# Layer 1's second product by 2x2 blocks in seven products, and attention by pairs of tiles

## The chip, the cores and the metric

The kernel runs on one core of a Trainium2 chip. Its time is the device time of one execution in microseconds: 808.15, the median of three runs (807.37 to 808.33). The engines are called as the profile calls them: PE (matrix products), PEld (its weight loads), DVE and ACT (elementwise work), POOL, and SP, which here issues all DMAs. TensorE's granted clock is at its upper level (2.4 GHz) in all but the very ends of the span.

## The reference

Attention within chunks of 64 tokens, and then two feed-forward layers on 2304 tokens:

```
scores = q k^T / 8  in chunks of 64;  attn = softmax(scores);  x = attn v   # 4 x 8 heads x 576 x 64 -> 2304 x 512
h = x @ w_in;   r = max(h, 0);   g = s*(r*r) + b;   y = g @ w_out           # layer 1: 512 -> 2048 -> 512
h = y @ w2_in;  g = max(h, 0) + log1p(exp(-|h|));   out = g @ w2_out        # layer 2, softplus
```

All is float32. The weights arrive as 64-bit words and are taken apart on the chip (`convert`: load, shift and mask on DVE, a linear step on ACT, three more on DVE).

## The kernel before

Precision. A float32 operand is split into a high part (rounded, ACT, line 584) and a low part (the rest, DVE, line 593). A product is three matmuls: high x high, high x low, low x high, each 128 x 128 by 384 columns.

Tiles. A tile is 128 tokens, a unit (u) two tiles, a group (j) three units, so a matmul's 384 columns are one group's half. `N` is 384.

First product of a layer (`quad`, PE at line 1000): by 2x2 blocks in seven products (Strassen's way with shared sums). For a pair of feature blocks `i` (8 of them) and a group `j` (3) a quad makes seven products of six matmuls; copies between PSUM banks on ACT (`seed`, 1022) and subtractions on DVE (571) stand between them. The four results pass relu or softplus (`hidden`, 1032) into places `go` in SBUF, from where they are stored.

Second product of layer 1 (`block`, PE at 1179): plain, six blocks of 16 features x 4 outputs x 3 matmuls. The features are loaded back (`hid`), squared on ACT (1148), scaled by s and shifted by b on ACT or DVE (436, 438), split, and multiplied. Second product of layer 2 (`second_by_blocks`, PE at 1335): seven products; for these a quad of layer 2 makes four sums of its results, stores seven blocks (`summed`), and `weights2` makes sums of the weights on POOL and stores them too (`forms2`).

Attention (`attention(t)`, one tile at a time): scores on PE (815, 64 columns of q against two heads' keys, where the keys of the other half are zeros), maximum on DVE, exp on ACT, in the first six tiles head by head with the sum beside it, division on POOL (899), transposes (915) and products with the values (934) on PE, and then the forms of a unit for the seven products.

Order. Nothing is scheduled by hand: `Work` takes every operation with a due time (`key`, corrected by the numbers of `TUNE`) and a cost, and writes one fixed order for each engine. Each engine then runs its list in order and waits on semaphores. Where the planner sees a gap of PE at the start, `warmed` puts in matmuls on zeros (line 1502).

Of the kernel before, what the change touches and what calls it, by code (L numbers as in the profile page):

```python
# [18 lines left out]
P = 128  # L19
# [18 lines left out]
ENDING = [(NF - 2, 0), (NF - 2, 1), (NF - 2, 2), (NF - 1, 2), (NF - 1, 0), (NF - 1, 1)]  # L38
ENDING_BY_GROUPS = [(c, j) for j in (2, 0, 1) for c in (NF - 2, NF - 1)]
BLOCKS = [4, 5, 0, 1, 2, 3]  # L40

EARLY = 6
# [10 lines left out]
B_AT = {1: 0, 2: 1, 3: 2, 5: 3, 6: 4, 7: 5, 4: 6}  # L53
# [19 lines left out]
AT_W2 = 0  # L73
AT_GH = 5 * XS
NGH = 4
AT_GL = AT_X2
NGL = 3
AT_Y = AT_GL + NGL * 4 * N

AT_V = AT_Y  # L80
NV = 12


TUNE = {
# [56 lines left out]
class Work:  # L141
# [11 lines left out]
    BYTES = 300e3  # L153
# [11 lines left out]
    def add(self, engines, key, emit, deps=(), uses=(), size=0, after=()):  # L165

        kind, self.nth = f"{self.part}.{self.nth}", self.nth + 1  # L170
        key += TUNE.get(self.turn, 0.0) + TUNE.get(kind, 0.0)
# [12 lines left out]

    def order(self, places):
# [14 lines left out]
        def earliest(op, e):  # L200
# [5 lines left out]
            for u in op.takes:  # L206
                t = max(t, min(free[u.kind].values(), default=float("inf")))
# [86 lines left out]
def block_attention_two_layers(  # L294
# [39 lines left out]
    if tc:  # L334
# [3 lines left out]
        operands = const.tile([P, AT_X2 + AT_WF - AT_W1], F32R, name="operands")  # L338
        shared = []
# [6 lines left out]
        nought = const.tile([P, P], F32R, name="nought")  # L346
        s_sb = const.tile([P, 1], F32, name="s_sb")
        b_sb = const.tile([P, 1], F32, name="b_sb")
        small = [
            [const.tile([P, H, 2], F32, name=f"{x}{i}") for x in ("mx", "sm")]  # L350
            for i in range(4)
        ]
        hid = [
            [dram.tile([P, NM, N], F32, name=f"hid{ph}_{x}") for x in range(2 * NG)]
            for ph in range(1)
        ]
        spill = [dram.tile([P, NM, DM], F32, name=f"spill{ph}") for ph in range(1)]
        summed = {
            (n, j): dram.tile([P, NF, N], F32, name=f"summed{n}_{j}")
# [3 lines left out]
        forms2 = dram.tile([P, 7, NF, 256], F32, name="forms2")  # L363

    def mem(a, n, v=None):

        if a < AT_X2:
            return operands[:, a : a + n].bitcast(F32)
        if a >= AT_WF:
            return plain[:, a - AT_WF : a - AT_WF + n]  # L370
        if a >= AT_W1:
            a -= AT_W1 - AT_X2
            return operands[:, a : a + n].bitcast(F32)
        while len(shared) <= v:
            kind = F32R if len(shared) % 2 else F32
# [1196 lines left out]
```

## Time and profile before

| | |
|---|---|
| median of three runs | 808.15 us |
| the profiled execution | 807.7 us |
| its span | 805.9 us |
| PE busy | 797.4 us, 5191 matmul records |
| DVE, ACT, POOL busy | 637.8, 510.1, 140.6 us |
| DMA | 180.28 MB, mean 224 GB/s |

PE's first attention matmul starts at 7.48 us, the first of a quad at 49.83, layer 1's second product at 249.92, layer 2's first matmul after it at 450.43, and the last matmul at some 801.6. Times of a row are the start and the length of an instruction or of a run of like ones; the next one can start before the last has ended, so a rate is read from starts. In rows of attention a matmul of the program shows as two records (float32 without the split).

### The profile page before, as it was taken

What the parts mean: (1) busy time and instruction counts of PE and PEld (TensorE: products, weight loads), DVE (VectorE), ACT (ScalarE), POOL (GpSimd) and SP (SyncE); (2) the same over time, 40 slices, a digit from 0 to 9 for tenths busy, and PEclk for the clock granted to TensorE, in tenths of its full rate; (3) what the DMA queues carried; (4) which work ended last, traced back from release to release, by engine and by line L of the source; (5) the groups of instructions that cost most, each with busy time, mean ns of one, the idle gap of its engine ahead of it and who ended that gap; (6) DMA issues with size and microseconds to landing.
All of it is one profiled execution on the core that took longest, in us unless ns stands there. A gap on an engine that the chain in (4) does not pass through costs nothing.

```text
span 805.9 us, 14677 instructions
## 1 busy us (share of the span) xinstructions
PE 797.4 (99%) x5191; PEld 780.1 (97%) x5191; DVE 637.8 (79%) x1166; ACT 510.1 (63%) x1085; POOL 140.6 (17%) x162
## 2 busy tenths in 40 slices
PE   8999999999999999999999999999999999999998
PEld 6788999999999999999999999999999999999997
DVE  5999898988868978889946786898865777778864
ACT  5756866666658777776676764655555566555553
POOL 3444411111110112222212320213100000000000
PEclk9999999999999999999999999999999999999999
DMA  8865367878769666777540056766778997678851
GB/s 256 248 179 160 138 210 261 278 245 274 246 227 383 235 202 194 253 222 252 166 136 29 30 191 212 260 227 225 256 261 286 345 347 241 233 236 289 282 176 60
DMA packets 80634, 180.28 MB, mean 224 GB/s; under 512 B 9008, under 2 KB 53040, under 8 KB 79664
## 3 DMA queue, kind: packets, MB, share of 16 engines
q1 hardware_dynamic: 80560, 179.34, 66.9%
q8 instruction: 41, 0.67, 0.4%
q14 instruction: 33, 0.27, 0.1%
HBM read 111.15 MB, written 68.16 MB: 222 GB/s over the span
## 4 chain that ended last, share of the span: by engine, by line
PE 95%; DVE 3%; ACT 1%; issue 0%; POOL 0%; ACTq 0%; POOLq 0%; DVEq 0%
PE at L1000 20%; PE S L1000 13%; PE at L1179 9%; PE S L1179 9%; PE A L1000 9%; PE S L1335 8%; PE at L1335 8%; PE A L1179 6%; PE A L1335 5%; PE S L1502 2%; PE at L934 2%; PE at L815 1%; PE at L915 1%; DVE operands L593 1%; ACT last L839 0%
## 5 line engine op out<-in xcount | busy, mean ns | idle before, releaser
L571 POOL TENSOR_TENSOR mem<-mem 128x256 f32<-128x256 f32 x120 | 104.8, 883 | 377.6 <-DVE mem L551 279.9
L593 DVE TENSOR_TENSOR operands<-mem,operands 128x384 fp32r<-128x384 f32 (+4 forms) x186 | 126.3, 695 | 38.4 <-ACT operands L584 36.8
L593 DVE TENSOR_TENSOR operands<-last,operands 128x384 fp32r<-128x384 f32 (+2 forms) x184 | 111.2, 625 | 46.7 <-ACT operands L584 39.7
L584 ACT CAST operands<-mem 128x384 fp32r<-128x384 f32 (+4 forms) x186 | 111.7, 621 | 55.6 <-PE at L1335 36.0
L584 ACT CAST operands<-last 128x384 fp32r<-128x384 f32 (+2 forms) x184 | 93.5, 528 | 57.8 <-PE S L1179 23.1
L1000 PE MATMUL at<-operands 128*128 128x384 f32 x624 | 120.1, 336 | 0.4 <-ACT S L1022 0.4
L1000 PEld LDWEIGHTS at<-operands 128*128 128x128 f32 x624 | 109.4, 188 | 0.8 <-ACT S L1022 0.7
L1335 PE MATMUL at<-operands 128*128 128x384 f32 x384 | 87.2, 334 | 0.0
L1335 PE MATMUL S<-operands 128*128 128x384 f32 x384 | 87.2, 334 | 0.0
L1179 PE MATMUL at<-operands 128*128 128x384 f32 x432 | 84.5, 335 | 0.9 <-ACT operands L584 0.8
L1000 PE MATMUL S<-operands 128*128 128x384 f32 x420 | 83.6, 336 | 0.0
L1179 PE MATMUL S<-operands 128*128 128x384 f32 x432 | 83.1, 334 | 0.0
L1179 PEld LDWEIGHTS at<-operands 128*128 128x128 f32 x432 | 75.5, 188 | 1.9 <-ACT operands L584 1.1
L1032 ACT ACTIVATE mem<-S 128x384 f32<-128x384 f32 x104 | 51.0, 492 | 38.8 <-PE S L1000 29.3
L1179 PEld LDWEIGHTS S<-operands 128*128 128x128 f32 x432 | 75.6, 188 | 0.0
L1000 PEld LDWEIGHTS S<-operands 128*128 128x128 f32 x420 | 73.6, 188 | 0.3 <-issue 0.2
L571 DVE TENSOR_TENSOR mem<-mem 128x384 f32<-128x384 f32 (+1 forms) x108 | 61.0, 573 | 14.3 <-ACT mem L1032 10.8
L1335 PEld LDWEIGHTS S<-operands 128*128 128x128 f32 x384 | 68.4, 188 | 0.0
L1335 PEld LDWEIGHTS at<-operands 128*128 128x128 f32 x384 | 68.4, 188 | 0.0
L1000 PE MATMUL at<-last,operands 128*128 128x384 f32 x336 | 65.7, 335 | 0.0
L1000 PE MATMUL A<-operands 128*128 128x384 f32 x300 | 60.2, 339 | 0.4 <-DVE A L571 0.4
L1000 PEld LDWEIGHTS at<-last,operands 128*128 128x128 f32 x336 | 58.8, 188 | 0.0
(80 smaller groups left out, 1226.1 us busy)
## 6 DMA issues: line engine op xcount, KB each, us to landing
mem<-in_w_dram SPq DMA_DIRECT2D x64, 512.0 KB, 4.6
summed<-mem SPq DMA_DIRECT2D x168, 192.0 KB, 2.5
mem<-summed SPq DMA_DIRECT2D x30, 768.0 KB, 5.5
hid<-mem SPq DMA_DIRECT2D x96, 192.0 KB, 3.0
last<-hid SPq DMA_DIRECT2D x24, 768.0 KB, 5.0
last<-summed SPq DMA_DIRECT2D x12, 768.0 KB, 5.2
mem<-forms SPq DMA_DIRECT2D x7, 1024.0 KB, 6.6
last<-in_q_dram SPq DMA_DIRECT2D x18, 256.0 KB, 4.7
```

The costliest lines, as they stand in the source:

```text
L571: lambda e: on(e).tensor_tensor(out=out(), in0=x(), in1=y(), op=op or ALU.subtract),
L584: lambda e: nc.scalar.copy(out=hi().bitcast(F32R), in_=x()),
L593: lambda e: nc.vector.tensor_tensor(out=lo().bitcast(F32R), in0=x(), in1=hi(), op=ALU.subtract),
L815: nc.tensor.matmul(out_[c * D : (c + 1) * D, pr], of("q")[:, pr * P + c * D : pr * P + (c + 1) * D], kb[:, :, pr, c, :], start=True, stop= ...
L915: nc.tensor.transpose(at(pt)[:, c], of("e")[:, c], ident)
L934: nc.tensor.matmul(at(px)[y, x], of("v")[y, x], of("aT")[y, x], start=True, stop=True)
L1000: nc.tensor.matmul(acc(dst)().rearrange("p (u c) -> p u c", u=GROUP), l[a], r[c], start=start and kk == 0 and x == 0, stop=kk == 1 and x == 2,
L1032: lambda e: nc.scalar.activation(out=at(go), in_=acc(place)(), func=AF.Softplus if ph else AF.Relu),
L1179: nc.tensor.matmul(at(accs[d])[:, :N], l[a], r[c], start=m == 0 and z == 0, stop=m == NM - 1 and z == 2,)
L1335: nc.tensor.matmul(at(accs[d])[:, :N], l[a], r[c], start=i == 0 and y == 0, stop=i == NF - 1 and y == 2,)
L1502: nc.tensor.matmul(x, nought, nought.unsqueeze(1).to_broadcast([P, KK, P]), start=True, stop=True)
```

## The change

Layer 1's second product uses `second_by_blocks` too, with seven products. `quad` makes squares (ACT) of its four results in layer 1 and then the four sums, on POOL for the first two feature blocks and on DVE for the rest; all seven blocks are stored. s is applied where results leave PSUM. b times the sum of the weights' columns is made by two columns of ones beside the first product's right operand (`more`), and added by ACT (`biased`). The weights' forms of layer 1 are made and stored as those of layer 2 are, the sums now on DVE. In the new quads the third and fourth sum are written over a feature, once that feature's store is through. `block`, `hid` and `spill` go away.

Attention runs by units: two tiles together, scores as 64 x 64 products in two PSUM banks, the first half of the heads of every unit with exp head by head. The low parts of six units' sums, 1024 wide, are made on POOL. In part of the weight conversions (`SIGNED`) ACT carries the sign through two steps, and DVE has one step less. Places in SBUF, `TUNE` and the lookahead are new, so every engine's order changes.

```diff
-ENDING = [(NF - 2, 0), (NF - 2, 1), (NF - 2, 2), (NF - 1, 2), (NF - 1, 0), (NF - 1, 1)]
...
-BLOCKS = [4, 5, 0, 1, 2, 3]
-
-EARLY = 6
+ENDING = [(c, j) for j in (2, 0, 1) for c in (NF - 2, NF - 1)]
+
+EARLY = [(u, 0) for u in range(9)]
+BY_PE = []
+LOW_BY_PE = []
+LOW_BY_POOL = range(6)
+SIGNED = [(0, 0), (0, 1), (1, 1)]
...
+SUMS_BY = ["POOL"] * 2 + ["DVE"] * 6
...
-    "attention 1": 3.5, "attention 14": 87, "attention 15": 11, "attention 16": -14, "attention 3": 6,
...
+    "attention 0": -425.5, "attention 0/0": -645, "attention 0/16": 5, "attention 1": -590.5,
...
-    BYTES = 300e3
+    BYTES = 330e3
...
+            if not ph:
+                o = add(
+                    {"ACT": act(N)},
+                    key + 0.1,
+                    lambda e: nc.scalar.activation(out=at(go), in_=at(go), func=AF.Square),
+                    [o],
+                    [go],
+                )
+            return go, o
...
+        t1 = Place(kinds[4])
+        t2, t4 = b11[0], b21[0]
+        e = "DVE" if ph else SUMS_BY[i]
...
+        o1 = sub(key, of(t1), of(b12), of(b11), N, [b12[1], b11[1]], [b12[0], b11[0], t1], e=e)
+        o3 = sub(key, of(b12), of(b22), of(b12), N, [o1, b22[1]], [b12[0], b22[0]], e=e)
+        o2 = sub(
+            key, of(t2), of(b12), of(b11), N, [o3, st1], [b12[0], b11[0], t2], ALU.add, e=e
+        )
+        o4 = sub(
+            key, of(t4), of(b21), of(t2), N, [o2, st2], [b21[0], t2, t4], e=e
+        )
...
+            def scores(e, t=t, primed=primed):
...
+                for pr in range(NP):
+                    for c in range(2):
+                        x = pr * P + c * D
+                        z = t * 256 + (pr % 2 * 2 + pr // 2) * D
+                        for hp in range(2):
+                            y = slice(hp * D, (hp + 1) * D)
+                            nc.tensor.matmul(
+                                at(scores_in[hp])[c * D : (c + 1) * D, z : z + D],
+                                of("q", t)[y, x : x + D],
+                                of("k", t)[y, x : x + D],
...
-                    r = [mem(*hi).bitcast(F32R), mem(*lo).bitcast(F32R)]
+                    r = [mem(hi[0], N + more, version).bitcast(F32R), mem(*lo, version).bitcast(F32R)]
...
+                                nc.vector.scalar_tensor_tensor(
+                                    out=a, in0=ps(), scalar=s_sb[:, 0:1], in1=b, op0=ALU.mult, op1=ALU.add
+                                )
...
-    for z, x in enumerate(BLOCKS):
-        block(0, x // 2, x % 2, end + z * dt, z == 0)
+    late = second_by_blocks(0, end)
```

The orders below are rows of one engine's list: line, operation, out<-in, width, and how many alike.

PE at the start. Before: scores at line 815, transposes 915, values 934, zeros 1502.

```order
L1502 MATMUL S_69<-nought 128x512 x3
L815 MATMUL at_72<-last_121 64x128 x8
L1502 MATMUL S_69<-nought 128x512 x8
L915 MATMUL at_70<-ident,last_121 128x128 x4
L1502 MATMUL S_69<-nought 128x512 x4
L815 MATMUL at_71<-last_121 64x128 x8
L934 MATMUL at_70<-last_121 64x64 x16
```

Now, at the first unit's transposes: scores at line 847, transposes 978, zeros 1566.

```order
L847 MATMUL at_72<-region_0_150 64x64
L847 MATMUL at_71<-region_0_150 64x64
L1566 MATMUL S_69<-nought 128x512 x4
L978 MATMUL at_70<-ident,region_0_143 128x128 x4
L1566 MATMUL S_69<-nought 128x512 x3
L978 MATMUL at_71<-ident,region_0_143 128x128 x4
L1566 MATMUL S_69<-nought 128x512 x6
```

A unit's two banks are transposed one after the other with zeros between. In all, zeros stand 74 times before and 113 times now, 71 and 110 of them ahead of the first matmul of a quad. Ahead of that matmul stand 11 tiles' scores, 9 tiles' transposes and values before, and five units (10 tiles) of each now.

DVE in layer 1's second product. Before: scale and shift (438), splits of features (593), conversions (479 to 551).

```order
L438 TENSOR_SCALAR last_2621<-last_2621,s_sb,b_sb 128x384
L593 TENSOR_TENSOR operands<-last_2621,operands 128x384 x2
L551 SCALAR_TENSOR_TENSOR mem<-mem 128x512
L479 TENSOR_SCALAR mem<-mem 128x512
L509 TENSOR_SCALAR mem<-mem 128x512
L537 SCALAR_TENSOR_TENSOR mem<-mem 128x512
L523 SCALAR_TENSOR_TENSOR mem<-mem 128x512
L593 TENSOR_TENSOR operands<-last_2621,operands 128x384 x2
```

Now: splits of weights and features (625), additions out of PSUM with s (1446), conversions (483 to 583).

```order
L625 TENSOR_TENSOR operands<-region_2_3305,operands 128x3x256
L625 TENSOR_TENSOR region_2_2993<-region_2_3305,region_2_2993 128x384 x4
L1446 SCALAR_TENSOR_TENSOR mem<-S_68,s_sb,mem 128x384
L625 TENSOR_TENSOR region_2_2993<-region_2_3305,region_2_2993 128x384
L1446 SCALAR_TENSOR_TENSOR mem<-at_70,s_sb,mem 128x384
L625 TENSOR_TENSOR region_2_2993<-region_2_3004,region_2_2993 128x384
L499 TENSOR_SCALAR mem<-mem 128x512
```

Additions and weights' splits have come between the features' splits. From the first take out of PSUM (1426) to the last addition (1446) there are 331 DVE instructions: 206 of width 384, 78 of 512 (26 of them TENSOR_SCALAR), 38 of 256, 7 of 768, 2 of 1024.

DVE late in layer 1's first product, with the semaphores that each row waits for (DMAHW is a DMA queue's). Before:

```order
L551 SCALAR_TENSOR_TENSOR mem<-mem 128x512 [waits DVE_49]
L571 TENSOR_TENSOR mem<-at_71,mem 128x384 [waits PE_49]
L479 TENSOR_SCALAR mem<-mem 128x512 [waits DMAHW1_49,DVE_49]
L509 TENSOR_SCALAR mem<-mem 128x512
```

Now: a quad's sums (603, 384 wide), weights' sums (603, 256 wide) and a conversion (583).

```order
L603 TENSOR_TENSOR mem<-mem 128x384 [waits DMAHW3_49,Activation_49]
L583 SCALAR_TENSOR_TENSOR mem<-mem 128x512 [waits DVE_49,Activation_49]
L603 TENSOR_TENSOR mem<-mem 128x384 [waits DVE_49]
L603 TENSOR_TENSOR mem<-mem 128x256 [waits DMAHW5_49]
L603 TENSOR_TENSOR mem<-mem 128x384 [waits DMAHW4_49,DVE_49]
L603 TENSOR_TENSOR mem<-mem 128x256
L603 TENSOR_TENSOR mem<-mem 128x384 [waits DMAHW7_49,DVE_49]
```

Sums of features stand where there were none, and each quad has some that wait for a DMA. By engine, the instructions of one execution go from 1168 to 1320 on DVE, 1039 to 1171 on ACT, 167 to 151 on POOL, 549 to 634 on SP.

## Rows read from the trace of the kernel before

**Rows 1.** The page: busy time by engine, and the chain that ended last.

```profile
PE 797.4 (99%) x5191; PEld 780.1 (97%) x5191; DVE 637.8 (79%) x1166; ACT 510.1 (63%) x1085; POOL 140.6 (17%) x162
...
PE 95%; DVE 3%; ACT 1%; issue 0%; POOL 0%; ACTq 0%; POOLq 0%; DVEq 0%
```

**Rows 2.** Busy by stretch, lines 1179, 1335: stretch, PE, PEld, clock, DMA share, GB/s.

```profile
249.00:451.00 202.00, 200.50 (x1152) 199.57 (x1152) 1.00 0.59 193
...
624.00:806.00 182.00, 175.21 (x1008) 174.76 (x1008) 1.00 0.72 246
```

**Rows 3.** Timeline of PE at the start: start us, length us, instructions.

```profile
30.95 1.89 PE L1502 MATMUL S<-nought 128*128 128x512 f32 x7
...
33.16 0.71 PE L1502 MATMUL S<-nought 128*128 128x512 f32 x2
33.81 1.09 PE L815 MATMUL at<-last 128*64 128x128 f32 x16
34.83 1.15 PE L934 MATMUL at<-last 64*64 64x64 f32 x32
35.91 0.49 PE L1502 MATMUL S<-nought 128*128 128x512 f32 x1
...
49.83 1.31 PE L1000 MATMUL A<-operands 128*128 128x384 f32 x6
```

**Rows 4.** Busy by stretch, line 1502 (matmuls on zeros), columns as Rows 2.

```profile
0.00:60.00 60.00, 22.16 (x74) 13.53 (x74) 1.00 0.80 228
```

**Rows 5.** Timeline of PE: the longest waits after the start, and the last matmuls.

```profile
249.92 0.44 PE L1179 MATMUL at<-operands 128*128 128x384 f32 x1 [0.78 <-ACT operands L584]
...
460.38 1.32 PE L1000 MATMUL at<-operands 128*128 128x384 f32 x6 [0.42 <-ACT S L1022]
...
463.10 1.33 PE L1000 MATMUL A<-operands 128*128 128x384 f32 x6 [0.36 <-DVE A L571]
...
801.28 0.69 PE L1335 MATMUL at<-operands 128*128 128x384 f32 x3
```

**Rows 6.** Timelines of DVE near 702 us and of ACT near 258 us.

```profile
700.62 0.56 DVE L593 TENSOR_TENSOR operands<-mem,operands 128x384 fp32r<-128x384 f32 x1 [0.48 <-ACT operands L584]
701.66 0.56 DVE L593 TENSOR_TENSOR operands<-mem,operands 128x384 fp32r<-128x384 f32 x1 [0.48 <-ACT operands L584]
702.14 0.55 DVE L571 TENSOR_TENSOR last<-S,last 128x384 f32<-128x384 f32 x1
702.61 0.55 DVE L571 TENSOR_TENSOR last<-at,last 128x384 f32<-128x384 f32 x1
...
257.93 0.52 ACT L584 CAST operands<-last 128x384 fp32r<-128x384 f32 x1
258.35 0.52 ACT L1148 ACTIVATE last<-last 128x384 f32<-128x384 f32 x1
```

**Rows 7.** Groups by line and shape: count, busy us, mean ns, idle before.

```profile
L593 DVE TENSOR_TENSOR operands<-last,operands 128x384 fp32r<-128x384 f32 x144 | 84.1, 601 | 35.7 <-ACT operands L584 34.7
...
L537 DVE SCALAR_TENSOR_TENSOR mem<-mem 128x512 uint32<-128x512 uint32 x64 | 45.6, 712 | 1.4 <-ACT mem L496 1.4
```

**Rows 8.** Busy by stretch: PE, PEld, DVE, ACT, POOL, clock, DMA share, GB/s.

```profile
100.00:150.00 50.00, 50.00 (x290) 49.99 (x289) 45.79 (x79) 31.91 (x63) 10.27 (x12) 1.00 0.72 237
...
250.00:300.00 50.00, 49.85 (x286) 49.59 (x287) 45.43 (x84) 41.05 (x86) 7.25 (x8) 1.00 0.72 252
```

**Rows 9.** Line 571 by engine: shortest, median, longest ns; first and last start us.

```profile
L571 POOL TENSOR_TENSOR mem<-mem x120: 725/908/1529, 11.8 to 584.4; 128x256 f32<-128x256 f32 x120
L571 DVE TENSOR_TENSOR mem<-mem x108: 409/555/1089, 74.7 to 633.0; 128x384 f32<-128x384 f32 x96, 128x256 f32<-128x256 f32 x12
```

**Rows 10.** DMA: page's 40 slices; 100 to 250 us (columns as Rows 2); landing of `hid`.

```profile
GB/s 256 248 179 160 138 210 261 278 245 274 246 227 383 235 202 194 253 222 252 166 136 29 30 191 212 260 227 225 256 261 286 345 347 241 233 236 289 282 176 60
...
100.00:250.00 150.00, 149.15 (x859) 148.81 (x857) 1.00 0.76 255
...
DMA to landing us min/median/max: 1.8/3.1/8.9
```

More of the change, by code (lines that the diff above doesn't have):

```diff
@@ L205, in earliest @@
                 t = max(t, d.start)
-            for u in op.takes:
-                t = max(t, min(free[u.kind].values(), default=float("inf")))
+            for x, u in enumerate(op.takes):
+                spots = sorted(free[u.kind].values())
+                nth = sum(o.kind == u.kind for o in op.takes[:x])
+                t = max(t, spots[nth] if nth < len(spots) else float("inf"))
             for u in op.gives:
@@ L456, in block_attention_two_layers, with convert @@
     turn = {}
-    def convert(ph, c, part, key, dst, uses=(), w=(), gone=()):
+    w2_gone = []
+    subtracted = []
+    w1_given = {}
+    def convert(ph, c, part, key, dst, uses=(), w=(), gone=(), ahead=False):
         chain = "f", part
@@ L473, in convert @@
         words = lambda: at(f).bitcast(U32).rearrange("p (a b) -> p a b", b=2)
-        a = lambda: at(am)[:, :DM].bitcast(U32)
-        m = lambda: at(am)[:, DM:].bitcast(U32)
+        a = lambda: at(am).bitcast(U32)
+        m = lambda: dst().bitcast(U32)
+        signed = (ph, part) in SIGNED and not (ph and c >= 2 * LATE)
         o1 = add(
@@ L568, in sub @@
         return add(
-            {e: pool(n) if e == "POOL" else dve(n, port=port)},
+            {z: pool(n) if z == "POOL" else dve(n, port=port) for z in e.split()},
             key,
@@ L577, in sub, with split @@
         )
-    def split(key, hi, lo, x, n, deps, uses=(), psum=False, r=(), wh=(), wl=()):
+    def split(key, hi, lo, x, n, deps, uses=(), psum=False, r=(), wh=(), wl=(), low="DVE"):
         o1 = add(
@@ L590, in split @@
         o2 = add(
-            {"DVE": dve(n, port=not psum)},
+            {low: pool(n) if low == "POOL" else dve(n, port=not psum)},
             key,
-            lambda e: nc.vector.tensor_tensor(
+            lambda e: on(e).tensor_tensor(
                 out=lo().bitcast(F32R), in0=x(), in1=hi(), op=ALU.subtract
@@ new lines, in slot, with parts @@
+        return (u // GROUP * 2 + h) * REGION + u % GROUP * 1792 + a * 256, n * 256
+    def parts(ph, u, key, at_, x, n, deps, uses=(), psum=False, r=()):
+        first, span, step = at_
+        cut = lambda h: lambda: mem(*slot(u, h, first, span), 1 + 2 * ph).rearrange(
+            "p (f g c) -> p f g c", g=2, c=P
+        )[:, ::step]
+        wh, wl = [[slot(u, h, z, 1) for z in range(first, first + span, step)] for h in range(2)]
+        low = "POOL" if ph == 0 and n == 4 and u in LOW_BY_POOL else "DVE"
+        return split(key, cut(0), cut(1), x, n * 256, deps, uses, psum, r=r, wh=wh, wl=wl, low=low)
@@ L768, in forms @@
[L768 to L790 removed]
+            ops += parts(ph, u, key + 0.1, (n, 2, 1), src, 2, done, uses, r=rw)
@@ new lines, in forms, with low_by_pe @@
+        return ops
+    def low_by_pe(u, key, at_, x, gone, place):
+        n = at_[1] * 256
+        hi, lo = slot(u, 0, *at_), slot(u, 1, *at_)
+        cut = lambda y: mem(*y, 1).rearrange("p (f g c) -> p f g c", g=2, c=P)
+        o1 = add(
+            {"ACT": act(n, True)},
+            key,
+            lambda e: nc.scalar.copy(out=cut(hi).bitcast(F32R), in_=x()),
+            gone[:1],
+            [place],
+            w=[hi],
+        )
+        o2 = add(
+            {"PE": mm(n)},
+            key,
+            lambda e: nc.tensor.matmul(
+                x(), minus_r, cut(hi).bitcast(F32R), start=False, stop=True, skip_group_check=True
+            ),
+            [o1, *gone],
+            [place],
+            r=[hi],
+        )
+        o3 = add(
+            {"ACT": act(n, True)},
+            key,
+            lambda e: nc.scalar.copy(out=cut(lo).bitcast(F32R), in_=x()),
+            [o2],
+            [place],
+            w=[lo],
+        )
+        return [o1, o3]
@@ new lines, in attention @@
+            if (u, hp) not in EARLY:
+                o5 = add(
+                    {"DVE": dve(DM, port=False)},
+                    key,
+                    lambda e, h=h, hp=hp: nc.vector.tensor_reduce(
+                        out=sm[:, h], in_=heads(of("e", hp)), op=ALU.add, axis=AX.X
+                    ),
+                    [o4],
+                    r=es,
+                )
+            o6 = add(
+                {"ACT": 0.12},
+                key,
+                lambda e, h=h: nc.scalar.activation(out=sm[:, h], in_=sm[:, h], func=AF.Identity, bias=1e-9),
+                [o5],
+            )
@@ new lines, in attention, with turned @@
+            last_small[u % 2, hp] = [o7]
+            def turned(e, hp=hp, pt=pt):
+                for y in range(NP):
+                    c = slice(y * P, (y + 1) * P)
+                    nc.tensor.transpose(at(pt)[:, c], of("e", hp)[:, c], ident)
+            o8 = add({"PE": 0.48}, key + 0.3, turned, [o7], [pt], r=es)
+            copied.append(
+                add(
+                    {"ACT": act(DM, True), "DVE": dve(DM, port=False)},
+                    key + 0.3,
+                    lambda e, hp=hp, pt=pt: copy(e, of("aT", hp), at(pt)),
+                    [o8],
+                    [pt],
+                    w=ts,
+                )
+            )
@@ new lines, in weights @@
+            pieces = ((0, 2), (2, 2), (4, 3), (7, 1))
+            loaded = {}
+            for a, m in pieces if x == 0 else ((0, NF),):
+                ld = load(
+                    key - 6 + a / 4,
+                    words(a, m),
+                    lambda a=a, m=m: forms2[ph][:, A_AT[n], a : a + m].rearrange("p a b -> p (a b)"),
+                    P * m * 1024,
+                    [o for i in range(a, a + m) for o in spilled[ph, i]] + (wf_last[ph] if x == 0 or ph else []),
+                    held,
+                    after=[gone] if gone else (),
+                    w=cells_of(a, m),
+                )
+                loaded |= {i: ld for i in range(a, a + m)}
@@ L1283, in weights @@
                     v2_ready[n, i] = ops
-            v2[n] = wp, apart
+            v2[n] = wp, apart, shared
+            if not ph and shared:
+                w1_given[1, x // 6] = ops
         def features(n, j, i0, key):
@@ L1446, in block_attention_two_layers @@
     times += [(t0, 1), (t0 + 7 * T, 1)]
-    for t in tiles:
-        attention(t, x_key(t))
-    another_use()
+    for u in range(NU):
+        attention(u, x_key(2 * u))
+    another_use(4, 5)
     for u in range(LAST, NU):
```

1089 lines of the change are left out of this document (510 added, 579 removed), and 69 rows, old and new, of the table TUNE.

## Prediction

> **What bounds the kernel now.** I read the page's busy times first: TensorE is busy 797.4 of 805.9 us, and the chain of work that ended last runs through PE for 95% [rows 1]. The difference of 8.5 us is 2.2 before the first matmul, 4.0 after the last one ends (801.28 + 0.69 = 801.97) and only 2.3 inside; the largest single waits are 0.78, 0.42 and 0.36 [rows 5]. The second view is the busy time by stage: layer 1's second product is 1152 matmuls in 200.50 us, layer 2's, already in seven products, 1008 in 175.21 [rows 2], so 0.174 us a matmul in both. The third is the timeline of PE in the first 60 us, where PE waits for attention and the gaps are filled with 74 matmuls on zeros (L1502) [rows 3, 4]. They hide nothing and are in-order work like any other: PE has no free time anywhere, so what PE executes is added up, and then the waits of PE that the change brings.
>
> **Part 1, the seven products.** They take 3 groups x 7 products x 8 features x 6 matmuls = 1008 in place of 1152, of the same width. This is what layer 2 does in 175.21 against 200.50 us: -25.3. In 92 of them two extra columns make the feature sums: 2/384 of 0.174 us each, 0.1 in all, left out.
>
> **Part 2, attention by units.** Transposes and value products keep their number on PE (72 and 288). Scores change shape: eight 64x128 per tile become sixteen 64x64. Eight took 34.83 - 33.81 = 1.02 us; sixteen value products, the nearest row of that shape, 35.91 - 34.83 = 1.08 [rows 3]. 18 tiles x 0.06 = +1.1. The order of PE holds 113 matmuls on zeros where it held 74. Seven in a row took 1.89, two 0.71, so one costs (1.89 - 0.71)/5 = 0.236 [rows 3], and 39 more +9.2. These are issued whether or not PE would have had to wait, so this cost is paid for certain unless the operands come later still. The first product on PE, at 49.83 now [rows 3], should move to about 59.
>
> **Part 3, what feeds PE.** Nothing here is on PE; it costs only where it makes PE wait. A 384-wide DVE operation is 0.55 us long, but the next may start 0.47 after it (702.14 to 702.61), and on ACT 0.42 (257.93 to 258.35) [rows 6]. So full load is reached when busy times sum to about 1.2 times the span.
> - Layer 1's first product. 96 squares move here from the second one: +96 x 0.42 = 40 us of ACT. The signed conversions of both weights (32) give one DVE operation of 0.712 [rows 7] to ACT: -32 x 0.71 x 0.47/0.55 = -19 on DVE and, at 0.42 x 512/384 = 0.56 each, +18 on ACT. 18 of the 24 quads make their four sums on DVE: 72 x 0.47 = +34; the 32 subtractions of 256 for the weights' forms leave POOL for DVE: 32 x 0.47 x 256/384 = +10. DVE +25, ACT +58 over some 175 us. In the row of 100 to 150 us DVE is busy 45.79 and ACT 31.91 of 50 [rows 8]; times 0.85 and 0.81 that is a load of 0.78 and 0.52, which becomes 0.92 and 0.85. PE is still the bound, with less cover: the seeds on ACT between two products of a quad now queue behind squares.
> - Layer 1's second product. From the first take to the last addition DVE has 331 instructions, by width 354.7 units of 384: 354.7 x 0.47 = 167 us; 26 of them are one-operand ones, whose 512 are some 0.2 us shorter, so 162. PE needs 20 x 48 x 0.174 = 167 for it. DVE has 5 us to spare in 167; before, it was busy 45.43 of 50 at this stage's start and PE lost under 1 us there [rows 8, 5]. Cover is thin here, and what goes late first is the low half of a split.
> - A new wait, in both layers. The third and fourth sum of a quad overwrite a feature in place, so they wait until that feature's store has landed; layer 2's had places of their own, layer 1 had no sums. Behind them on DVE stand splits and the subtractions that seed the next product. Stores in layer 1 landed in 1.8 / 3.1 / 8.9 us (min, median, max) [rows 10]. The order puts other work between, enough for 3 us, not for 9.
> - SP issues 85 more DMAs, on a queue that is not what PE waits for in any row of [rows 5].
>
> I take +4.0 us for all these waits together: between -2.3 (those inside the span vanish) and +18 (the first rival), nearest to the rows of [rows 5], some three times their sum, because DVE and ACT each come to within about a tenth of full in layer 1.
>
> **POOL.** It now makes six lows of 1024 and 24 sums of 384, and gives up 41 of 256. A 256-wide one took 0.73 to 1.53 us, a DVE operation of the same line up to 1.09 with a median of 0.56 [rows 9]: the two engines do lengthen each other. The Trainium skill, "SBUF — State Buffer", section "SBUF: two separate sides", says that DVE with two SBUF inputs and GpSimd share one port pair that is locked for a whole instruction, the loser fully blocked. The stretched maxima agree. By that rule a 1024-wide low blocks DVE for all of its length, which is the second rival below.
>
> **Sum.** The profiled execution took 807.7 (span 805.9 and 1.8 around it). 807.7 - 25.3 + 9.2 + 1.1 + 4.0 = 796.7. The median of the runs, 808.15, is 0.45 above the profiled one, so 797.1; I say 797.
>
> **Rivals.**
> 1. Slower: DVE bounds layer 1's second product. Its splits of 384 took 0.601 us on average in this very stage [rows 7], and if each holds DVE that long (it waits for ACT's high half, whose ends come 1.04 us apart at 700.62 and 701.66 [rows 6]), 161 of them cost 0.13 more each: 162 + 21 = 183 against 167, +16, of which 2 are already counted: 811. It decides from 0.50 a split on, where the 5 us to spare are gone, and at 0.57 the gain is gone. For it: the thin cover. Against: the same splits run back to back elsewhere at 0.47, and DVE ran near full at 250 us without holding PE.
> 2. The head. Scaled by width a 1024-wide POOL low takes 4 x 0.73 = 2.9 to 4 x 1.53 = 6.1 us [rows 9]. Three of them stand ahead of the first product, in units 0 to 2; at the long end on all three 3 x 3.2 = 9.6, half of it likely: 797 + 5 = 802. For it: DVE and POOL were both busy there. Against: other warm-up matmuls cover part.
> 3. DMA. 72 more stores of 192 KB (14.2 MB) and 7.3 MB of forms for 4.2 of spilled weights add 17.3 MB to the stage in which the DMA engines were 0.76 busy at 255 GB/s [rows 10]. Over 170 us (43.4 MB now) that is 357 GB/s; at 255/0.76 = 336 it takes 60.7 MB / 336 = 181 us, some +10: 807, no measurable change. Against: single slices ran at 383 [rows 10], and weights can be fetched earlier.
> 4. The change brings only what PE's count says, no new wait: 797 - 4 = 793.
>
> **Chances.** A difference under 0.2%, 1.6 us, cannot be told from no change here. Forecast with case 4 (791 to 801.5): 0.68. Rival 2 (801 to 806): 0.13. Rival 3 (804 to 809): 0.10, half of it faster. Rival 1 (809 to 815): 0.09. Faster 0.68 + 0.13 + 0.05 = 0.86, same 0.05, slower 0.09. Range 791 to 808; the likeliest case's own is 791 to 801.5.
>
> **What would show it.** Right: 2016 seven-product matmuls in two stages of 175 us each; the first product at 58 to 60 us; PE idle inside the span 4 to 9 us, scattered over layer 1, released by ACT or DVE. The first rival: PE waits for the low halves by DVE, with DVE over 95% busy, all through layer 1's second product. The second: PE waits beyond the zeros before 60 us, released by POOL's lows. The third: DMA share over 95% and stores landing in 6 us or more in layer 1's first product, with ACT or DVE waiting for them. I am wrong altogether if a matmul of the new stage takes more than 0.174 us without a wait, or if the gaps of the head shrink in spite of the zeros.

## The result, and the profile after

The changed kernel takes 816.41 us (median of 4 runs, 814.69 to 818.0) against 808.24 for the kernel before on the same chip: a ratio of 1.0098 [1.0075, 1.0121]. It is slower by 1%, outside the predicted range. The profiled execution is at 815.57 us, with a span of 813.8.

The page: busy times, and the engines of the chain that ended last; these answer to [rows 1].

```profile
PE 785.0 (96%) x5374; PEld 758.0 (93%) x5374; DVE 688.1 (85%) x1318; ACT 551.2 (68%) x1241; POOL 151.9 (19%) x146
...
PE 58%; DVE 8%; ACT 3%; DMA 2%; issue 1%; POOL 0%; ACTq 0%
```

TensorE's busy time fell by 12.4 us (797.4 to 785.0) and the span rose by 7.9. PE carries 58% of the span where it carried 95%. The chain as the profile follows it back ends at 220.8 us and covers some 72% of the span, so most of that fall is time not followed; of what it covers PE has about 0.8, and DVE, ACT and DMA have most of the rest.

The two second products by stretch, line 1362, columns as [rows 2].

```profile
265.00:451.00 186.00, 178.07 (x1008) 175.50 (x1008) 1.00 0.80 285
631.00:814.00 183.00, 177.41 (x1008) 177.11 (x1008) 1.00 0.70 238
```

1008 matmuls in each, as counted, but 177 to 178 us in place of 175. The start of PE's timeline, up to the first quad (scores at 847, values at 1005, zeros at 1566, first product at 1073), answers to [rows 3]; the row behind it, of the zeros by stretch, to [rows 4].

```profile
43.86 1.16 PE L847 MATMUL at<-region 64*64 64x64 f32 x64
44.95 0.96 PE L1566 MATMUL S<-nought 128*128 128x512 f32 x3
...
50.04 1.16 PE L1005 MATMUL at<-region 64*64 64x64 f32 x64 [1.26 <-DVE region L440]
51.13 1.32 PE L1073 MATMUL A<-region,operands 128*128 128x384 f32 x6
```

```profile
0.00:60.00 60.00, 32.52 (x113) 21.35 (x113) 1.00 0.68 230
```

The first quad starts 1.3 us later than before, not 9. The six largest of PE's waits from 50 to 262 us follow, longest in total first: line that waited <- releaser: us in total, times, longest. They answer to [rows 5].

```profile
PE A L1073 <- DVE A L603: 2.5, 2, 1.7
PE at L1073 <- ACT S L1095: 2.4, 2, 2.1
PE A L1073 <- ACT S L1095: 2.4, 2, 2.1
PE S L1073 <- ACT S L1095: 1.8, 3, 0.7
PE at L847 <- DVE mem L603: 1.7, 1, 1.7
PE at L1005 <- DVE region L440: 1.3, 1, 1.3
```

Single waits of 2 us, where 0.78 was the longest: PE waits for seeds (1095, ACT) and for the subtractions that seed (603, DVE). By stretch, all engines, columns as [rows 8], the first row for 100 to 250 us:

```profile
100.00:250.00 150.00, 139.60 (x763) 134.30 (x762) 131.34 (x248) 122.82 (x260) 40.06 (x39) 0.99 0.88 297
100.00:150.00 50.00, 46.12 (x246) 44.05 (x244) 41.22 (x70) 38.18 (x81) 23.81 (x22) 0.97 0.78 254
250.00:300.00 50.00, 47.22 (x258) 44.47 (x257) 38.02 (x73) 36.75 (x81) 0.00 (x0) 1.00 0.98 355
```

and the same for the kernel before, in a row not shown so far:

```profile
100.00:250.00 150.00, 149.22 (x860) 148.89 (x858) 126.42 (x219) 97.39 (x192) 22.73 (x28) 1.00 0.76 255
```

In this stretch DVE went up by 5 us, ACT by 25, DMA from 255 to 297 GB/s, and PE fell from 860 matmuls to 763.

**Where the time went.** Take the start of each matmul of the two products and the start of the next. The usual spacing is 0.173 us. What a spacing has over that is a wait where it is over 0.2 us, and a slower pitch where it is below.

| stage, us | before | after | waits before, after | slower pitch before, after |
|---|---|---|---|---|
| to the first quad | 49.8 | 51.1 | | |
| layer 1, both products | 400.6 | 399.4 | 2.9, 26.5 | 0.5, 3.6 |
| layer 2, both products | 351.2 | 359.5 | 1.4, 5.4 | 0.5, 4.9 |
| last matmul starts at | 801.6 | 810.1 | | |

Of the 26.5, 17.6 lie in layer 1's first product from 100 us on (0.9 before), 3.4 ahead of that, 5.5 in the second. So layer 1 gave back in waits all that it saved, and layer 2, which was not to change, lost 8.3.

### The profile page after: what moved, and what is told of

Read it like the earlier page. It is cut to its first block, busy times and chain, and to the rows that moved or that the text cites. A ratio compares the mean times of both kernels' runs of the same rounds, so it can differ in the third digit from the quotient of the medians.

```text
span 813.8 us, 15584 instructions
## 1 busy us (share of the span) xinstructions
PE 785.0 (96%) x5374; PEld 758.0 (93%) x5374; DVE 688.1 (85%) x1318; ACT 551.2 (68%) x1241; POOL 151.9 (19%) x146
## 4 chain that ended last, share of the span: by engine, by line
PE 58%; DVE 8%; ACT 3%; DMA 2%; issue 1%; POOL 0%; ACTq 0%
PE S L1362 15%; PE at L1362 15%; PE at L1073 11%; PE A L1362 10%; PE S L1073 5%; PE A L1073 3%; DVE mem L603 2%; DVE region L625 2%; DMA summed<-mem 2%; ACT region L616 1%; DVE operands L625 1%; DVE mem L569 0%; DVE mem L514 0%; ACT mem L1105 0%; ACT S L1095 0%
## 5 line engine op out<-in xcount | busy, mean ns | idle before, releaser
L1073 PE MATMUL at<-region,operands 128*128 128x384 f32 x960 | 186.4, 340 | 5.7 <-ACT S L1095 4.6
L603 POOL TENSOR_TENSOR mem<-mem 128x256 f32<-128x256 f32 (+1 forms) x109 | 111.5, 1034 | 390.2 <-DVE mem L583 304.3
L1073 PEld LDWEIGHTS at<-region,operands 128*128 128x128 f32 x960 | 168.9, 188 | 10.6 <-ACT S L1095 8.2
L616 ACT CAST region<-mem 128x384 fp32r<-128x384 f32 (+3 forms) x210 | 110.1, 533 | 71.7 <-PE at L1362 44.8
L625 DVE TENSOR_TENSOR region<-mem,region 128x384 fp32r<-128x384 f32 (+2 forms) x204 | 112.5, 564 | 34.9 <-ACT region L616 33.7
L625 DVE TENSOR_TENSOR region<-region,region 128x384 fp32r<-128x384 f32 (+3 forms) x206 | 113.9, 571 | 23.8 <-ACT region L616 22.5
L1073 PE MATMUL S<-region,operands 128*128 128x384 f32 x624 | 127.0, 342 | 3.5 <-ACT S L1095 2.9
L1073 PEld LDWEIGHTS S<-region,operands 128*128 128x128 f32 x624 | 111.6, 190 | 6.0 <-ACT S L1095 4.2
L1362 PE MATMUL S<-region,operands 128*128 128x384 f32 (+1 forms) x504 | 116.2, 338 | 0.4 <-DVE region L625 0.4
L1362 PE MATMUL at<-region,operands 128*128 128x384 f32 (+1 forms) x504 | 115.7, 338 | 0.0
L1362 PEld LDWEIGHTS S<-region,operands 128*128 128x128 f32 x504 | 90.5, 188 | 0.7 <-DVE region L625 0.7
L1362 PEld LDWEIGHTS at<-region,operands 128*128 128x128 f32 x504 | 90.7, 188 | 0.0
L1095 ACT COPY S<-at 128x384 f32<-128x384 f32 x80 | 37.9, 474 | 22.5 <-PE at L1073 19.8
```

Source lines behind the costliest of these rows:

```text
L603: lambda e: on(e).tensor_tensor(out=out(), in0=x(), in1=y(), op=op or ALU.subtract),
L616: lambda e: nc.scalar.copy(out=hi().bitcast(F32R), in_=x()),
L625: lambda e: on(e).tensor_tensor(out=lo().bitcast(F32R), in0=x(), in1=hi(), op=ALU.subtract),
L1073: nc.tensor.matmul(acc(dst)().rearrange("p (u c) -> p u c", u=GROUP), l[a], r[c], start=start and kk == 0 and x == 0, stop=kk == 1 and x == 2,
L1095: lambda e: nc.scalar.copy(out=acc(place)(), in_=acc(ba)()),
L1362: nc.tensor.matmul(at(accs[d])[:, : N if c else N + more], l[a], r[c], start=i == 0 and y == 0, stop=i == NF - 1 and y == 2,)
```

## The experiments

All times are medians beside the kernel before on the same chip. "Waits" are those of layer 1's first product from 100 us on, "pitch" the median spacing of first-product matmuls, both in the profiled execution; DVE and ACT are busy times from 100 to 250 us. The waits are of one execution each, and executions of one changed kernel can differ by 9 us (e11: 808.5 to 817.29), so a difference of 1 to 3 us in waits decides nothing by itself. e2 to e5 and e8 to e10 leave out part of the computation or store other values.

| kernel | us | ratio to before | waits | pitch | DVE, ACT |
|---|---|---|---|---|---|
| before | 808.2 | 1 | 0.9 | 0.173 | 126, 97 |
| after | 816.4 | 1.0098 [1.0075, 1.0121] | 17.6 | 0.175 | 131, 123 |
| e1_shift | 811.6 | 1.0046 [1.0028, 1.0064] | 17.9 | 0.173 | 133, 124 |
| e1_both | 818.7 | 1.0124 [1.0095, 1.0153] | 21.5 | 0.175 | |
| e7_before_apart | 814.8 | 1.0073 [1.0051, 1.0095] | 1.3 | 0.175 | |
| e2_no_square | 813.7 | 1.0077 [1.0048, 1.0105] | 14.5 | 0.175 | 135, 97 |
| e3_half_stores | 845.2 | 1.0456 [1.0402, 1.051] | 18.4 | 0.175 | 131, 123 |
| e4_short_sums | 809.4 | 1.0009 [0.9994, 1.0024] | 18.2 | 0.173 | 115, 124 |
| e5_free_stores | 811.5 | 1.0033 [1.0016, 1.0049] | 16.9 | 0.173 | 135, 125 |
| e6_sums_dve | 812.0 | 1.0032 [1.0015, 1.005] | 21.0 | 0.173 | 134, 122 |
| e8_no_forms | 806.5 | 0.998 [0.9963, 0.9998] | 15.5 | 0.173 | 94, 110 |
| e9_no_extras | 799.0 | 0.9883 [0.9858, 0.9909] | 7.5 | 0.173 | 75, 84 |
| e10_no_holds | 802.5 | 0.9924 [0.99, 0.9949] | 9.2 | 0.173 | 75, 83 |
| e11_forms_pool | 811.9 | 1.0047 [1.0024, 1.007] | 20.1 | 0.173 | 129, 123 |
| e12_squares_pool | 823.1 | 1.0183 [1.0168, 1.0198] | 31.1 | 0.173 | 134, 103 |
| e13_before_act | 821.4 | 1.0163 [1.0148, 1.0179] | 10.6 | 0.173 | 123, 126 |
| e14_before_both | 845.0 | 1.0453 [1.0434, 1.0472] | 32.5 | 0.173 | 137, 109 |

### The pitch: three kernels with bytes left empty

The lines of the second product of the changed kernel, by where the two operands lie (left operand last in `out<-in`); shortest, median and longest record in ns.

```profile
L1362 PE MATMUL S<-region,operands x504: 332/337/442, 266.0 to 808.6; 128*128 128x384 f32 x154, 128*128 128x386 f32 x14
...
L1362 PE MATMUL S<-region,region x192: 331/334/443, 278.7 to 424.7; 128*128 128x384 f32 x192
```

Weights in `operands` and features in a region: 337 ns and a spacing of 0.175 (mean 0.176). Both in regions: 334 and 0.173. In the changed kernel `operands` starts 128 bytes past a multiple of 512 in the partition, the regions on one.

```diff
+        gap = const.tile([P, 32], F32, name="gap")   # e1_shift: ahead of the regions
+        gap = const.tile([P, 96], F32, name="gap")   # e1_both: ahead of operands, everything moves
```

> The changed kernel with 128 unused bytes ahead of the region tiles; order and work are the same. Theory 1 (place): a matmul whose weights lie in the operands tile and whose right side lies in a region takes 0.1757 us and not 0.173 because of where the two lie to each other; in the kernel before both lay alike to a multiple of 512 bytes (both at 128), now at 128 and 0. It expects 0.173 us a matmul, 3000 x 0.0025 = 7 us less: 809. Theory 2 (traffic): other engines' accesses to the same tiles slow these matmuls. It expects no change: 816.

> The changed kernel with 384 unused bytes ahead of all tiles: operands and regions move together, the operands tile now starts at a multiple of 512 bytes. Theory 1 (how the two lie to each other) expects no change: 816, 0.1757 us a matmul. Theory 1b (the weights' own place counts) expects 809. Theory 2 (traffic) expects no change.

With 128 bytes between them e1_shift gains 4.9 us; its pitch is 0.173 (0.174 in one group) and its slower pitch 1.4 us in all, against 8.5. The same line there:

```profile
L1363 PE MATMUL S<-region,operands x504: 332/334/446, 264.3 to 804.3; 128*128 128x384 f32 x154, 128*128 128x386 f32 x14
```

In e1_both all tiles moved together, and nothing was gained. The converse, the kernel before with its weights 128 bytes further on (and 384 unused bytes behind them):

```diff
-            a -= AT_W1 - AT_X2
+            a -= AT_W1 - AT_X2 - 32
```

> The kernel before with its weights' places moved 128 bytes up and 384 unused bytes behind them, so that the weights lie 128 bytes further on, modulo 512, from the first and second group's features than they did, as in the changed kernel. Instructions and their order stay. If the distance of weights and moving side in a partition sets the matmul's pitch, the median spacing goes from 0.173 to 0.175 us or more in the first products, and the time rises by 3 to 9 us, to 811 to 817. If what made the changed kernel's matmuls slower was something else (its new regions, its DMA traffic), the spacing stays 0.173 and the time 808.

The order is untouched, and the time goes up by 6.2 us. Where weights of `w1` are the left operand the records become 337 ns; layer 1's plain second product stays at 334. First the row of the kernel before, then the two of e7:

```profile
L1000 PE MATMUL at<-operands x624: 333/334/443, 136.3 to 624.8; 128*128 128x384 f32 x156
```

```profile
L1001 PE MATMUL at<-operands x624: 334/337/440, 137.8 to 630.0; 128*128 128x384 f32 x156
...
L1180 PE MATMUL at<-operands x432: 331/334/441, 252.9 to 453.3; 128*128 128x384 f32 x144
```

So where weights and right side lie in relation to each other set the pitch. It explains 5 to 7.5 of the lost us, and none of the waits.

### The waits: one suspect at a time

First in the changed kernel itself, squares left out on ACT (`lambda e: None`), and stores of half the partitions.

> The changed kernel without the 96 squares (left out of the computation), all else in the same order. PE loses 19.7 us by waits over 0.2 us between matmuls of layer 1's first product from 100 to 279 us. Theory A (ACT's load makes the seeds late): 40 us of ACT go, the waits fall to 7 or less, 12 us faster: 804. Theory B (DMA): features still leave no faster, the waits stay over 15: 813 to 816.

> The changed kernel where layer 1 stores only 64 of 128 partitions of each block of features (as many DMAs, half the bytes, 16.5 MB less from 60 to 280 us) and loads those rows twice; so half the tokens' features are not the reference's. Theory B (the DMA engines, 0.92 to 0.98 busy in that stage, land stores late and hold the places that ACT needs): landing falls under 3 us, the waits to 7 or less, 12 us faster: 804. Theory A (ACT): waits stay over 15, 813 to 816.

Without squares ACT has the load of the kernel before (97 us), and PE still waits 14.5 of 17.6 us. With half stores the DMA share in the stage falls from 0.88 to 0.73, the median landing of `summed` from 60 to 275 us from 4.3 to 3.0 us, and the waits are 18.4:

```profile
100.00:250.00 150.00, 140.28 (x759) 135.23 (x758) 131.03 (x248) 122.86 (x260) 40.22 (x39) 0.98 0.73 218
```

So neither carries the waits alone, and taking traffic away took no wait away. (The 29 us of e3 fall later, in the second product, where the halved loads run at a DMA share of 0.99 and 269 GB/s from 250 to 300 us.) What follows stands on e1_shift.

```diff
# e4: three of the four sums
-        o3 = sub(key, of(b12), of(b22), of(b12), N, ...
+        o3 = sub(key, cut(b12), cut(b22), cut(b12), N, ...   # o2, o4 too; cut: 8 columns
# e5: stores of products 1 and 2 read `ident`
# e6: sums of the first six blocks
+            lambda e: on(by or e).tensor_tensor(             # by="DVE"
```

> The changed kernel with the 128 unused bytes of the first experiment, and in layer 1's first product three of the four sums of a block (o3, o2, o4) are made over 8 columns instead of 384, so their results are left out; every wait, store, place and position stays. The quantity is the sum of TensorE's waits over 0.2 us between the matmuls of layer 1's first product (from 100 us to its end), which is 17.9 us with the sums whole and 0.9 us in the kernel before. Theory B (VectorE, 88 to 92 per cent busy there, is late because of the sums' work, and what it is late with holds ScalarE and TensorE): under 9 us, and the time falls by 8 us or more, to some 803. Theory A (the 384-column places are held until a store has landed, and o2 and o4 wait for landings at the head of VectorE's queue): 15 us or more and no gain above 3 us. Theory C (the sums of the first six blocks on GpSimd at 1.1 us each): the waits before 155 us go (some 6 us), those after it stay.

> The changed kernel with the 128 unused bytes, and two of the seven stores of each block of layer 1's first product (products 1 and 2) read a constant tile instead of the block's place, so what they store is not the feature; number, size, queue position and destination of the transfers stay, but neither o2, o4 nor the next block waits for these two to land. Theory A (places held by landings): the waits in layer 1's first product fall from 17.9 us to under 9, the time by 8 us or more. Theories B (VectorE's load) and C (GpSimd's sums): 15 to 19 us, and the time within 2 us of 811.5.

> The changed kernel with the 128 unused bytes, and the sums of the first six blocks of layer 1's first product, which GpSimd makes at 1.1 us each, are issued at the same places of the order on VectorE at 0.47 us. Theory C: the waits before 155 us fall from some 7 us to under 2, the time by 4 to 6 us. Theory B: VectorE carries 24 instructions more, 11 us, between 95 and 150 us, and the waits there stay or grow. Theory A: no change above 2 us.

All three theories fall as sole causes: 18.2, 16.9 and 21.0 us of waits. The hold of the third and fourth sum by a landing, the new wait that I had named, is worth 1 us of waits and nothing in the time (811.5 against 811.6); e6 moved work from POOL to DVE and gained nothing. e4 gained some 2 us, which its profile does not show in these waits; the profiled execution, at 811.9, was among its slowest.

### The waits: all added work, and the same work in the kernel before

```diff
+        if left_out[0] and "SP" not in engines:   # e8: in weights2(0, i);
+            emit = lambda e: None                 # e9: squares and o3, o2, o4 too; e10: stores read `ident`
```

> The changed kernel with the 128 unused bytes, and the conversion and the sums that make the block forms of layer 1's second weights are left out (all that VectorE and ScalarE do for them in layer 1's first product); their loads and stores stay, with what lies in the place. The quantity is the sum of TensorE's waits over 0.2 us in layer 1's first product: 17.9 us with everything, of it 6.0 before 125 us. Theory D (these conversions stand at the head of VectorE's and ScalarE's queues, wait there for 512 KB loads, and the seeds and subtractions that TensorE needs are queued behind): the waits after 125 us fall from 11.9 us to under 4, the time by 6 us or more, to 805 or less. Theory E (ScalarE's and VectorE's added work as a whole has used up the slack that hid each delay, so that none of its parts alone decides): waits of 10 to 15 us in all, 2 to 5 us of time. Theory F (the order itself, the positions at which seeds and products stand, makes the waits whatever the added work costs): 15 us or more.

> As e8, and in layer 1's first product the squares on ScalarE and three of the four sums of a block on VectorE and GpSimd are left out as well, so that ScalarE and VectorE carry there no more than in the kernel before; stores, loads, places and every position stay. Theory E: the waits in layer 1's first product fall from 17.9 us to under 6 and the time to 803 or less. Theory D: as in e8, within 3 us. Theory F: the waits stay above 12 us.

> As e9, and all seven stores of a block in layer 1's first product read a constant tile, so that no place there is held by a landing; the transfers stay in number, size, queue position and destination. If holds matter once the added work is out of the way, the waits fall by another 3 us or more against e9; by theories D, E and F they are within 2 us of e9's. What is left here is the order's own.

The weight forms alone take 2.4 us of waits away (theory D wanted 8) and 5 us of time, squares 3 of either (within the spread), sums none of the waits and 2 us of time; all together 10.4, and 12.5 us of time. That is theory E in kind, though 7.5 us stay where under 6 were expected. e10 gains nothing on e9; the constant tile is read in short pieces, so its transfers take longer (DMA share 0.98 at 303 GB/s against 0.96 at 326), and that part stays inconclusive.

Now the reverse. The kernel before keeps its order, and gets one more ACT instruction behind each feature, then three more of DVE a block.

```diff
+                    None if ph else nc.scalar.activation(out=at(go), in_=at(go), func=AF.Relu),
+        again = lambda: nc.vector.tensor_tensor(out=at(dd), in0=at(dd), in1=at(dd), op=ALU.max)
+        sd.emit = lambda e: [subtract(e), *([] if ph else [again() for z in range(3)])]
```

> The kernel before, with one more ScalarE instruction behind each of the 96 features of layer 1's first product (the ramp again, in place, which changes no value), 0.43 us each, some 41 us: ScalarE's load becomes that of the changed kernel, VectorE's stays. In the kernel before ScalarE waits for TensorE for 39 us there, in the changed one for 8. Theory E: ScalarE's slack pays for most of it, and the waits of TensorE go from 0.9 to 1 to 5 us, the time up by 1 to 4 us. Theory F (the order's positions): within 1 us of 808.5.

> As e13, and behind the last subtraction of each of the 24 blocks three more instructions of VectorE over 128x384 (the larger of a value and itself, in place, which nobody reads), 0.47 us each, 34 us in all. Theory E: with the slack of both engines gone TensorE waits more than the sum of the two would cost alone: 6 to 18 us in layer 1's first product, the time 814 to 826. Theory F: under 3 us.

```profile
100.00:250.00 150.00, 145.60 (x818) 141.13 (x817) 122.98 (x210) 125.58 (x258) 24.82 (x30) 1.00 0.68 233
```

```profile
100.00:250.00 150.00, 132.81 (x720) 123.33 (x718) 137.23 (x241) 109.38 (x225) 22.36 (x26) 1.00 0.61 205
```

The first row is e13's: with ACT at 126 us, the kernel before, order unchanged and with less DMA traffic, loses 13 us, three times what was expected. The second is e14's: 137 and 109 us in a stretch in which PE does 720 matmuls, and 36 us lost, twice the most expected. The load of the two feeding engines makes such waits without any new order (theory F as the sole cause falls). None of PE's waits in e13 is put down to the ramps, the old or the added ones, so it is not that they hold a bank. How the load does it is seen in what ACT waits for from 100 to 250 us, first before, then after, then in e13.

```profile
ACT mem L1032 <- PE S L1000: 13.3, 23, 1.4
ACT S L1022 <- PE at L1000: 8.1, 16, 0.6
ACT mem L496 <- DVE mem L479: 6.7, 12, 1.5
ACT mem L429 <- PE at L1000: 6.1, 10, 1.6
...
ACT S L1022 <- PE A L1000: 3.4, 6, 0.6
```

```profile
ACT mem L1105 <- POOL mem L603: 6.5, 4, 2.7
ACT mem L532 <- DVE mem L514: 5.8, 4, 3.0
ACT mem L438 <- PE A L1073: 1.9, 1, 1.9
...
ACT S L1095 <- PE at L1073: 0.8, 2, 0.4
```

```profile
ACT S L1022 <- PE at L1000: 2.1, 4, 0.6
```

Before, ACT stood 39 us waiting for PE (13.3 + 8.1 + 6.1 and smaller ones): for 22 of the 40 seeds of this stretch it stood ready when the product ended. After, it waits for PE some 8 us, and for POOL and DVE some 15, and is ready for 2 seeds of 37; in e13, where only its load was raised, for 4 of 39. It is behind PE, and so a delay of ACT or DVE can reach PE through the next seed: seeds (ACT S L1095) end the larger part of the waits of PE listed above.

Last, two attempts to move load to POOL, idle for 42 of 50 us from 150 us on.

> The changed kernel with the 128 unused bytes, and the 32 sums that make the block forms of layer 1's second weights are issued on GpSimd (0.82 us each) at the same places of the order in VectorE's stead (0.36 us each). GpSimd is busy 8 of 50 us there. Theory E (ScalarE's and VectorE's added work together has used up the slack): 11.6 us less on VectorE, the waits of layer 1's first product 17.9 to 15 or 17, the time 1 to 2 us lower, 809.5 to 811. Theory F (positions alone): 811.5. A loss would mean that the stores of the forms, now later, hold a place that a load needs.

> As e11, and two of a block's four squares (b11 and b21, from the third strip of columns on: 36 instructions) go from ScalarE at 0.43 us to GpSimd at about 1.1 us. ScalarE carries 15 us less. Theory E: another 1 to 3 us, 807 to 810, near the kernel before. Rival: GpSimd's 1.1 us and its hand-overs make the sums o1 to o4 and their stores later, and the gain is lost, 811 to 814.

Neither did what was expected. e11 changed nothing that can be measured. In e12 ACT is 20 us lighter and PE waits 13 us more: the sums of the next weights queue on POOL behind squares, and ACT waits for them at the head of its own queue.

```profile
ACT operands L617 <- POOL mem L604: 10.6, 5, 4.9
```

No kernel that computes everything beat the kernel before.

## Why the prediction was wrong, step by step

**Part 1, -25.3: right in count.** 1008 matmuls stand where 1152 stood. Without waits and at a pitch of 0.173 they would take 175.

**Not seen: the pitch, some +7.5** (3.1 in layer 1, 4.4 in layer 2). I took 0.174 us a matmul over from [rows 2] as if it belonged to the shape. It belongs to the places too, and the change moved those. My own sign "more than 0.174 us without a wait" came true; e1_shift and e7 show the cause.

**Part 2, +10.3 forecast, +1.3 measured.** The zeros cost about what I said (113 take 32.52 us of busy time, 74 took 22.16 [rows 4]), but I priced the new scores by values of a form of before. From start to start 64 records of a unit's scores now take 1.09 us (43.86 to 44.95), and so do 64 of values (50.04 to 51.13), for two tiles; before, one tile's values took 1.08 for 32 records and its scores 1.02 [rows 3]. Up to 60 us scores are busy 7.74 us where they were 14.01, values 4.65 (256 records) where they were 12.05 (338). That paid for the zeros. The error was in the change's favour, by luck. The Trainium skill, "TensorEngine Tiling (Array Packing)", section "Overview", says that the array can work as four independent tiles of 64 x 64. The trace fits that, without proving it: 17 ns a record in the new order, in which neighbouring products lie in different tiles, 34 in the order before.

**Part 3, +4.0 forecast, +27.6 measured** (23.6 in layer 1, 4.0 in layer 2); here the prediction failed. I forecast loads of 0.92 on DVE and 0.85 on ACT for layer 1's first product, noted that "the seeds on ACT between two products of a quad now queue behind squares", and then read the loads as cover: PE still the bound, so a tenth to spare is enough. That tenth was not there. A row's busy time counts time in which instructions overlap only once: 1152 matmuls, each 0.334 us long, are 385 us, and their row says 200.50 of 202 [rows 2]. So DVE's 45.79 and ACT's 31.91 of 50 us [rows 8] are loads of 0.92 and 0.64 as they stand. I multiplied them by 0.85 and 0.81 for overlaps that were out already; with my own additions they come to 1.06 and 0.97. The trace has, from 100 us to the start of the second product:

```profile
100.00:266.00 166.00, 155.28 (x846) 148.75 (x845) 144.55 (x274) 135.27 (x287) 40.06 (x39) 0.99 0.89 301
```

For nearly the same products DVE and ACT needed 126 and 97 us before; 144.55 and 135.27 are 0.96 and 0.90 of the 150 us that PE took for them then. And even a mean load well below 1 says how much work fits, not when it is done: e2 has 0.90 and 0.64, and 14.5 us of waits. The rows that would have told were those of ACT waiting for PE, 39 us of 150, and the change, by my own count, asked for 58 us more of ACT and 25 of DVE. My bound of +18 came from the second product alone; the term has exceeded it by 10.

In the 26.5 us, 2.8 are the clock. PE's granted clock fell to its lower level (1.2 GHz) twice, from 73 us on, amid waits of 0.8 and 1.7 us, for some 7 us, and from 110.4 us on, after one of 2.1 us, for some 3; 19 matmuls came at 0.32 us in place of 0.173 (19 x 0.147). The stretches before and behind the second fall:

```profile
106.00:110.30 4.30, 2.19 (x14) 1.86 (x12) 4.08 (x6) 4.27 (x11) 2.07 (x3) 1.00 0.55 196
110.30:113.30 3.00, 3.00 (x10) 3.00 (x11) 0.00 (x0) 0.80 (x2) 2.77 (x4) 0.52 0.88 253
```

**The rivals.** The first, DVE in layer 1's second product: no; it is busy up to 49.77 of 50 us there, yet that product's waits are 5.5 us, over two thirds of them before 290 us. The second, POOL's lows in the head: the waits of PE before 60 us are put down to DVE, none to POOL. The third, DMA in layer 1's first product: its marks are there (share 0.92 and 0.96 from 150 to 250 us; landings of `summed` in 1.8 / 4.4 / 10.6 us over both layers, min, median, max), but e3 brought the share down to 0.73 and PE waited as long. At the start of the second product the chain of waits names a DMA for 8.35 us, a store of features (`DMA summed<-mem`, from 268.33 us). It did not hold ACT, which had no idle time there: it came from ramps and squares (1116) straight to the splits of the weights' forms (616), whose loads had landed by 273.9 us, and PE waited 1.7 us behind these splits. First ACT, then PE:

```profile
276.23 0.53 ACT L1116 ACTIVATE mem<-mem 128x384 f32<-128x384 f32 x1
276.66 1.12 ACT L616 CAST region<-region 128x256 fp32r<-128x256 f32 x2
```

```profile
278.66 0.61 PE L1362 MATMUL S<-region,region 128*128 128x384 f32 x2 [1.54 <-ACT region L616]
```

The fourth, no new wait: no. The sum as measured: -25.3 + 1.3 + 27.6 + 7.5 = +11.1, against +8.5 from last matmul to last matmul; the 2.6 between them I have not split. They lie in layer 1, where the attention of the last units runs between the first quads.

**What stays open.** At about the load of the kernel before on both engines (e2: 135 and 97 us), the changed order waits 14.5 us where the old one waits 0.9; with far less (e9) still 7.5. So the load is not the whole cause. Whether the rest is the order's own or the landings', no run settles: in e9 ACT stands 8.0 us waiting for stores to land (ACT mem L1112 <- DMA summed<-mem, 8 times), and e10, which takes that hold away, waits 9.2 us with slower transfers. Nor did a run take away the weights' loads that DVE waits for, 9.2 us from 100 to 250 us (5.8 before; the longest 3.6 and 1.9). And the parts do not add: ACT's 40 us cost 13 in the kernel before and gave back 3 in the changed one.

## What to carry to other kernels

Before giving a feeding engine more work, read how long it waits for the engine it feeds: that wait is the slack, and once it is spent delays of the feeder reach the bound engine, though the feeder is 82 or 88% busy. Take the busy time of a stretch as the load it is: overlaps are out of it already. Leaving out one added piece of work at a time can show nothing where the pieces act jointly; leave out all of them, or add the load to the old kernel. When a change moves tiles in SBUF, compare the spacing of matmuls of one shape before and after, and shift a tile by 128 bytes before anything else is blamed.

## What the runs showed of the hardware

A matmul of 384 columns came every 0.173 us or every 0.175 to 0.176, by where its two operands lie in the partition in relation to each other, weights 128 bytes further on, modulo 512, being the slower case and no distance the faster; some 3300 matmuls lie so in the changed kernel, and 0.0025 each makes 8 us. The Trainium skill, "TensorE: Matmul & The Clock Gate", section "Wait — 56ns, not 53.3ns?", gives columns over the clock and 2.5 ns more, 162.5 ns for 384 at 2.4 GHz as an estimate from it. At the upper level the measured 173 and 175 decide. For the lower level that section of the Trainium skill gives columns over 1.2 GHz, 320 ns as an estimate from it; the trace shows 0.32 us. Products of 64 x 64 ran at 17 ns a record when neighbours in the order used different quarters of the array (64 in 1.09 us), and at 34 ns in the order before (32 in 1.08); no run varied this by itself.
